# RWKV attention and squared-ReLU FFN: the first chunk's loads with pieces outermost, a permuted identity, and ten fillers at the start

## The chip, the cores and the metric

The kernel runs on one core of a Trainium2 chip. The metric is device time in microseconds, the median of several executions. The core has TensorE (matmuls, in the profile PE and PEld), VectorE (DVE), ScalarE (ACT), GpSimd (POOL) and SyncE (SP), which issues most DMAs; sixteen DMA engines move the data.

## The reference

Per batch and head a state of 48 by 48 runs over 768 tokens; its output, laid out as tokens by 384, goes through a feed-forward network (FFN) with a squared ReLU. All is float32; there are 4 batches and 8 heads.

```
for t in range(S):
    cur = einsum('bhd,bhe->bhde', u[None] * k_t, v_t)
    y[:, :, t] = einsum('bhd,bhde->bhe', r_t, state + cur)
    state = w_t[:, :, :, None] * state + einsum('bhd,bhe->bhde', k_t, v_t)
x = y.transpose(0, 2, 1, 3).reshape(B * S, H * D)
out = square(maximum(x @ w_in, 0)) @ w_out      # 384 -> 2048 -> 384
```

## The kernel before

The tokens go in six chunks of 128. A unit is one chunk of one batch, so chunk 0 has four units. For each unit `attention` forms running products of w (the scans, L509), scaled r and k, scores, and the output; `ffn` then takes a chunk of all four batches through 16 slices of the hidden dimension (first matmuls L688, second L706). Weights come from DRAM in 8 groups (`load_w`, L391 and L393) and are split into a high and a low part by ScalarE, VectorE and GpSimd (`split_w`, L404 to L425).

In the first chunk w, k and r are loaded one batch at a time (L444): twelve loads, each with 128 partitions of 8 tokens x 48 numbers, 1536 bytes. The partition is 16 * head + piece, where a piece is 8 consecutive tokens. TensorE turns each loaded tile into rows of head dimension by columns of tokens (`turn`, L497): 16 matmuls per tile, the loaded data stationary, the columns of an identity moving, picked per pair of heads (`pick`). A profile shows each of them as two records. The three turns of the first unit are queued in the order w, k, r; behind them on TensorE stands a turn of the second unit. VectorE's scans read the turned w, its products at L529 and L520 the turned k and r, and the rest of its queue follows in order. In later chunks the data is turned on VectorE (L459) instead, and spread by DMAs (L469).

Everything after the setup is added to a `Plan`, which simulates the engines with given costs, orders the steps by their simulated starts, and then writes them out in that order. No step is reordered by the hardware: each engine works its queue off in order. At most eight DMAs are in flight in the plan. Before a TensorE step that the simulation has waiting, `run` puts fillers (L750): transposes of the identity into a free bank, whose number is computed from the simulated idle time (`IDLE`, `s.fill`). Fillers take no time in the simulation.

The first planned TensorE step is the transpose of u (L359), which has no simulated dependence, but on the chip waits for a small DMA that ScalarE's queue issues (L357). The first turn comes after it. The lines of the count are:

```
if at < self.IDLE[0] and bank is not None:
    s.fill = max(0, int((at - max(idle, self.IDLE[1]) - self.IDLE[2]) / self.IDLE[3])), bank
```

Of the kernel before, what the change touches and what calls it, by code (L numbers as in the profile page):

```python
# [9 lines left out]
F32 = mybir.dt.float32  # L10
# [25 lines left out]
class Plan:  # L36
# [8 lines left out]
    QUEUES = {"sp": 0.5, "actq": 0.36}  # L45
    LANES, RUNS, SLACK, START = 8, 2300, 2.0, 1.4
    SWITCH, KEEP = 0.094, 1.0
    IDLE = (110.0, 2.8, 0.3, 0.12)
    filler, RULE = None, 1

    def __init__(self):
        self.steps, self.pools, self.last, self.readers = [], {}, {}, {}
# [26 lines left out]
    def order(self):  # L79
# [13 lines left out]
        while len(out) < len(self.steps):  # L93
# [40 lines left out]
            if unit == "pe":  # L134
                bank = next((x[1] for p in ("a", "hp") for x in self.pools.get(p, ()) if x[0] <= idle), None)
                if at < self.IDLE[0] and bank is not None:
                    s.fill = max(0, int((at - max(idle, self.IDLE[1]) - self.IDLE[2]) / self.IDLE[3])), bank
            wait[s.engine].remove(s)
# [43 lines left out]
        return sorted(out, key=lambda s: (s.at, s.n))  # L182

    def run(self):
        for s in self.order():
            for _ in range(s.fill[0] if self.filler else 0):
                self.filler(s.fill[1])
            s.fn()
# [39 lines left out]
def kernel(  # L228
# [12 lines left out]
    V, A, G, T = nc.vector, nc.scalar, nc.gpsimd, nc.tensor  # L241
    A.preload_act_table_set("natural_log_exp_and_others")
    B, H, S, D = r.shape
# [3 lines left out]
    NP = H // 2  # L247
# [10 lines left out]
    def place(name, shape, dtype, at):  # L258
        n = 1
        for x in shape[1:]:  # L260
            n *= x
        if at is None:
            nc.alloc_sbuf_tensor(name + "_place", [128, n], F32)
            at = placed[name] = nc.sbuf_base - 4 * n
        return nc.alloc_sbuf_tensor_at(name, shape, dtype, offset=at).ap()
# [13 lines left out]
    spare, spare2 = placed[f"ro{NG - 2}"], placed[f"ri{NG - 2}"]  # L279
    sel = place("sel", [HP, KT, J], F32, spare)  # L280
    last_y = [place(f"ly{i}", [HP, C], F32, spare + 768 + 512 * i) for i in range(2)]
    first_v = [place(f"v0{i}", [128, H * J], F32, at) for i, at in enumerate((spare + 1792, spare + 3840, spare2, spare2 + 2048))]
    gts = []
    for i in range(3):
        g = place(f"g{i}", [128, 2, 512], F32R, None)
# [9 lines left out]
    ident = const.tile([128, 128], F32, name="ident")  # L295
# [14 lines left out]
    TB = C // 16  # L310
# [34 lines left out]
    for q in range(KT):  # L345
        for h, i in enumerate(SIDE[q]):
            x = sel[:, q, h * D:h * D + PC]
# [19 lines left out]
    P.add("pool", 1.0, RANKS.unit(0, 3, "load") + 0.5, lambda: G.tensor_scalar(out=un, in0=un, scalar1=-1.0, scalar2=None, op0=ALU.mult), w=["un"])  # L367
    for t in Ss:
        V.memset(t, 0.0)

# [58 lines left out]
    def attention(c, b, rank):  # L431
        ss = slice(c * C, c * C + C)
# [4 lines left out]
        if b % 2 == 0:  # L437
            st = Slot("st" if c else "st0", n)
            both[n] = d = {"st": st}
            after = [both[n - 1]["z"]] if n > 2 else []  # L440
            for b0 in (b, b + 1) if c == 0 else ():
                for i, src in ((0, w), (2, k), (1, r)):
                    def load(i=i, src=src, b0=b0):
                        nc.sync.dma_start(out=st.tile.rearrange("s (t b x) -> s t b x", t=3, b=2)[:, i, b0 - b, 0:TB * D],  # L444
                                          in_=src[b0, :, ss, :].rearrange("h (a s) d -> h a (s d)", s=TB))
                    P.add("sp", 0.65, rank("load") + b0 - b, load, w=[(st, b0 - b, i)], after=after, runs=128)
            for b0, m in ((b, 2),) if c else ():
                for i, src in ((0, w), (2, k), (1, r)):
                    def load(i=i, src=src, b0=b0, m=m):
                        nc.sync.dma_start(out=st.tile.rearrange("s (t b h d) -> s t (b h) d", t=3, b=2, h=H)[:, i, (b0 - b) * H:(b0 - b + m) * H, 0:D],  # L450
                                          in_=src[b0:b0 + m, :, ss, :].rearrange("b h s d -> s (b h) d"))
                    P.add("sp", 1.05 * m, rank("load") + b0 - b, load, w=[(st, x, i) for x in range(b0 - b, b0 - b + m)], after=after, runs=128 * H * m)
            if c > 0:
                z = Slot("st", n)

                def blocks(i):
                    zt = z.tile.rearrange("a (u t p q i) -> a u t p q i", u=2, t=3, p=NP, q=3)
                    sv = st.tile.rearrange("s (t b p q x) -> s t b p q x", t=3, b=2, p=NP, q=3)
                    V.transpose(out=zt[:, i].rearrange("a t p q i -> a t (p q) i"),  # L459
                                in_=sv[:, :, i].rearrange("s t p q x -> s t (p q) x"))  # L460

                for i in range(2):
                    d["z"] = P.add("dve", 1.3, rank("z"), lambda i=i: blocks(i), r=[(st, i, x) for x in range(3)], w=[(z, i)])
                used = [s for s in P.steps if any(type(x) is tuple and x[:2] == ("pt", n % 2) for x in s.keys)]

                def spread(q, x, m, to, tb):
                    zz = z.tile.rearrange("a (w q i) -> a q w i", w=6 * NP, q=3)
                    pz = pts[n % 2].rearrange("a u t p s -> a (u t p) s")
                    nc.sync.dma_start(out=pz[to:to + m, :, 32 * tb:32 * tb + 32], in_=zz[32 * tb + x:32 * tb + x + m, q])  # L469

                for q, x, m, to in ((0, 0, 32, 0), (1, 0, 16, 32), (1, 16, 16, 64), (2, 0, 32, 80)):
                    for tb in range(4):
                        P.add("sp", 0.62 * m / 32, rank("pt"), lambda a=(q, x, m, to, tb): spread(*a), r=[(z, 0), (z, 1)],
                              w=[("raw", n, q, x, tb)], after=used, runs=24 * m)
        d = both[n]
# [7 lines left out]
                                                              in_=v[b, :, ss, :].rearrange("h s d -> s h d")), w=[vt], runs=128 * H)  # L483
        if c == 0:
            home = (["o0", "o1", "o2"], ["o3", "hp", "hp"], ["o2", "o3", "a"], ["o2", "o3", "a"])[b]
            ps = {}
            for i, h in zip((0, 2, 1), (home[0], home[2], home[1])):
                ps[i] = Slot(h) if h in ("hp", "a") else ("ob", int(h[1]))

                def turn(i=i):  # L490
                    to = tl(ps[i]).rearrange("a (p x y) -> a p x y", p=NP, y=TB)
                    rows = st.tile.rearrange("s (t b x) -> s t b x", t=3, b=2)[:, i, ui]
                    pick = ident.rearrange("s (p j x) -> s p j x", p=NP, j=2)
                    for y in range(TB):
                        for j in range(2):
                            n = (J, D)[j]
                            T.matmul(to[j * J:j * J + n, :, :, y], rows[:, y * D:y * D + n], pick[:, :, j], start=True, stop=True, skip_group_check=True)  # L497
                P.add("pe", 1.0, rank("turn"), turn, r=[(st, ui, i)], w=[ps[i]], mode=3)

            def tl(x):  # L500
                return x.tile if type(x) is Slot else obs[x[1]]
            src = lambda t: tl(ps[t]).rearrange("a (p s) -> a p s", p=NP)[0:HP]
        else:
            src = lambda t: pt[:, t]
# [133 lines left out]
        for nm, sl, y, hi, lo, k1, c1, c2 in outs:  # L638
            P.add("act", c1, rank(nm), lambda y=y, hi=hi: A.activation(hi(), y(), AF.Copy, scale=-1.0), r=[sl], w=[k1 + ("hi",)], after=freed)  # L639
            P.add("dve", c2, rank(nm), lambda y=y, hi=hi, lo=lo: V.scalar_tensor_tensor(  # L640
                out=lo(), in0=y(), scalar=-1.0, in1=hi().bitcast(F32), op0=ALU.mult, op1=ALU.subtract), r=[sl, k1 + ("hi",)], w=[k1 + ("lo",)])
# [86 lines left out]
    x = 0  # L728
    for c in range(NC):
# [4 lines left out]
        order = [(f, bs) for bs in ((0, 2), (2, B)) for f in range(HALF[c])] + [(f, (0, B)) for f in range(HALF[c], NF)]  # L734
# [23 lines left out]
    with tc.If(any_bad > 0):  # L758
        with tc.tile_pool(name="dram", bufs=1, space=bass.MemoryType.DRAM) as dr, \
                tc.tile_pool(name="slow", bufs=1) as sl:  # L760
            TB = 8
# [6 lines left out]
            with tc.For_i(0, S, TB) as t0:  # L768
# [17 lines left out]
                for b in range(B):  # L786
                    nc.sync.dma_start(
                        out=xd[b * S:b * S + S].rearrange("s (h d) -> h s d", d=D)[:, ds(t0, TB)],
                        in_=ys[b * H:b * H + H])
# [58 lines left out]
```

## Time and profile before

| what | us |
|---|---|
| median of three timed executions | 547.25 (546.74 to 547.51) |
| span of the profiled execution, first to last instruction | 545.6 |
| busy TensorE (PE) | 530.7, 97% |
| busy VectorE | 351.2, 64% |
| busy ScalarE | 300.4, 55% |
| busy GpSimd | 92.8, 17% |

The profile gives the profiled execution by its span; a whole time of that one execution isn't listed, so the span is set beside the median, 1.65 us above it. The page cuts the span into 40 slices and gives each engine's busy share in tenths. TensorE is at 9 in all slices but the first and the last, fillers included. VectorE and ScalarE are near 8 or 9 in the first ten or so, and lighter later. DMA is at 9 and below in the first third. In rows of the timeline the first number is the start, the second the duration, then engine, line, operation, tiles and count; a bracket gives the idle time before and what ended it. A line of SPq is the issue of a DMA, not its transfer.

### The profile page before, as it was taken

The page shows a single profiled execution, that of the slowest core. Times are in us where ns is not written, and L with a number is a line of the kernel's source. Part 1 is how long each engine was busy: PE and PEld are TensorE (multiplying, and loading weights), DVE is VectorE, ACT ScalarE, POOL GpSimd, SP SyncE. Part 2 cuts the span into 40 slices and gives each one's busy share as a digit, 9 for nine tenths or more (in the row PEclk, how much of TensorE's full clock was granted, in tenths as well). Part 3 has the DMA queues.
Part 4 walks back from the last instruction along what each step waited for, and adds up shares of the span by engine and source line. Part 5 has one row for each costly group of instructions (what it writes and reads, how often), then busy time and mean ns, then how long its engine had stood idle before and what let it go on. Part 6 is the DMA issues. An engine that isn't in the chain of part 4 may idle for free.

```text
span 545.6 us, 11056 instructions
## 1 busy us (share of the span) xinstructions
PE 530.7 (97%) x4250; PEld 470.7 (86%) x4250; DVE 351.2 (64%) x652; ACT 300.4 (55%) x728; POOL 92.8 (17%) x111
## 2 busy tenths in 40 slices
PE   5999999999999999999999999999999999999994
PEld 5888998889998989888888888889888998999994
DVE  2999888989796959696784684948443333333331
ACT  2887989895766675483834377464333232333221
POOL 2036533634030311212030030200000000000000
PEclk9999999999999999999999999999999999999997
DMA  4999695657947587674577155770011000000001
GB/s 150 231 246 234 136 257 143 138 106 110 183 75 113 115 89 124 82 155 59 91 119 110 26 104 101 123 95 1 0 44 44 1 0 1 29 31 0 1 0 62
DMA packets 195817, 50.91 MB, mean 93 GB/s; under 512 B 183984, under 2 KB 190640, under 8 KB 195760
## 3 DMA queue, kind: packets, MB, share of 16 engines
q1 hardware_dynamic: 195440, 49.76, 46.7%
q8 instruction: 35, 0.57, 0.5%
q10 hardware_dynamic: 320, 0.40, 0.2%
q14 instruction: 22, 0.18, 0.1%
HBM read 31.66 MB, written 4.72 MB: 67 GB/s over the span
## 4 chain that ended last, share of the span: by engine, by line
PE 90%; DMA 5%; SPq 1%; DVE 1%; ACT 1%; issue 0%; DVEq 0%
PE hp L688 38%; PE ob L706 38%; PE a L607 4%; PE a L567 4%; DMA ri<-in_moe_w_in_dram 3%; PE a L599 2%; PE a L659 2%; PE a L579 1%; DMA st<-in_k_dram 1%; SPq L444 1%; DMA st<-in_r_dram 1%; ACT m L556 0%; SPq L391 0%; PE a L621 0%; DVE m L571 0%
## 5 line engine op out<-in xcount | busy, mean ns | idle before, releaser
L706 PE MATMUL ob<-wo,g 128*128 128x384 f32 x1152 | 226.9, 341 | 0.0
L688 PE MATMUL hp<-x,wi 128*128 128x512 f32 (+1 forms) x1062 | 222.8, 355 | 0.0
L706 PEld LDWEIGHTS ob<-wo,g 128*128 128x128 f32 x1152 | 200.1, 188 | 10.3 <-issue 2.6
L688 PEld LDWEIGHTS hp<-x,wi 128*128 128x128 f32 x1062 | 173.9, 188 | 26.5 <-DVE g L700 1.0
L693 ACT ACTIVATE t<-hp 128x512 f32<-128x512 f32 (+1 forms) x118 | 61.1, 518 | 122.3 <-PE hp L688 107.7
L697 DVE SCALAR_TENSOR_TENSOR hp<-hp,t 128x512 f32<-128x512 f32 (+1 forms) x96 | 58.1, 606 | 90.9 <-ACT t L693 90.7
L700 DVE TENSOR_TENSOR g<-hp,g 128x512 fp32r<-128x512 f32 (+1 forms) x118 | 68.9, 584 | 38.0 <-ACT g L699 37.1
L699 ACT CAST g<-hp 128x512 fp32r<-128x512 f32 (+1 forms) x118 | 59.7, 506 | 52.9 <-DVE hp L697 52.5
L556 ACT ACTIVATE m<-ident,beta 128x128 f32<-128x128 f32 x192 | 60.6, 397 | 1.2 <-DVE beta L541 1.1
L571 DVE COPY_PREDICATED m<-caus,a 128x512 f32<-128x512 uint8 x48 | 34.1, 732 | 6.2 <-PE a L567 5.0
L640 DVE SCALAR_TENSOR_TENSOR x<-a,x 112x128 fp32r<-112x128 f32 (+2 forms) x64 | 20.6, 344 | 24.6 <-ACT x L639 23.0
L509 DVE TENSOR_TENSOR_SCAN pt<-pt,zero 112x128 f32<-112x128 f32 x80 | 30.0, 421 | 4.0 <-DMA pt<-st 3.5
L639 ACT ACTIVATE x<-a 112x128 fp32r<-112x128 f32 (+2 forms) x64 | 18.5, 323 | 21.0 <-PE a L607 16.6
L567 PEld LDWEIGHTS a<-pt 48*128 48x128 f32 x384 | 24.0, 187 | 6.7 <-issue 2.9
L567 PE MATMUL a<-pt 48*128 48x128 f32 x384 | 28.9, 285 | 0.7 <-DVE pt L546 0.7
L607 PE MATMUL a<-m,v 128*48 128x128 f32 (+1 forms) x384 | 26.9, 279 | 0.4 <-DVE m L571 0.2
L538 POOL TENSOR_TENSOR st<-st 128x384 f32<-128x384 f32 x20 | 20.9, 1050 | 37.4 <-DVE st L459 37.4
L459 DVE STREAM_TRANSPOSE st<-st 128x1152 f32<-128x1152 f32 x20 | 26.3, 1350 | 0.0
L607 PEld LDWEIGHTS a<-m,v 128*48 128x48 f32 (+1 forms) x384 | 19.8, 128 | 5.7 <-issue 4.2
L525 POOL COPY Ec<-pt 112x4 f32<-112x4 f32 x20 | 6.0, 300 | 103.8 <-DVE pt L509 103.8
L425 POOL TENSOR_TENSOR wi<-q,wi 128x768 fp32r<-128x768 f32 x8 | 16.7, 2087 | 28.5 <-ACT wi L424 23.3
L540 POOL TENSOR_TENSOR st<-st,un 128x384 f32<-128x384 f32 x20 | 21.3, 1071 | 1.3
(95 smaller groups left out, 428.2 us busy)
## 6 DMA issues: line engine op xcount, KB each, us to landing
pt<-st SPq DMA_DIRECT2D x80, 96.0 KB
ro<-in_moe_w_out_dram SPq DMA_DIRECT2D x8, 768.0 KB
v<-in_v_dram SPq DMA_DIRECT2D x24, 192.0 KB
st<-in_w_dram SPq DMA_DIRECT2D x10, 384.0 KB
st<-in_k_dram SPq DMA_DIRECT2D x10, 384.0 KB
st<-in_r_dram SPq DMA_DIRECT2D x10, 384.0 KB
pt<-st SPq DMA_DIRECT2D x80, 48.0 KB
out_dram<-q SPq DMA_DIRECT2D x20, 192.0 KB
```

The costliest lines, as they stand in the source:

```text
L459: V.transpose(out=zt[:, i].rearrange("a t p q i -> a t (p q) i"), in_=sv[:, :, i].rearrange("s t p q x -> s t (p q) x"))
L509: lambda p=p: V.tensor_tensor_scan(out=pt[:, 0, p], data0=src(0)[:, p], data1=zero.broadcast_to([HP, C]), initial=1.0, op0=ALU.mult, op1=A ...
L556: A.activation(mv(j)[:, p], ident, AF.Copy, scale=beta.tile[:, 2 * p + j:2 * p + j + 1])
L567: T.matmul(mts[j].tile.rearrange("s (p t) -> s p t", p=NP)[:, p], pt[js, 2, p], pt[js, 1, p], start=True, stop=True)
L571: lambda j=j: V.copy_predicated(out=mv(j), mask=caus.unsqueeze(1).broadcast_to([128, NP, C]), data=mts[j].tile.rearrange("s (p t) -> s p t ...
L607: T.matmul(spot(p)[to:to + n + D], vt.tile[:, o - n:o + D], mv(j)[:, p], start=(c == 0 and p == SPLIT), stop=True, skip_group_check=True)
L688: T.matmul(hp.tile[:, 0:n], wi[f][:, wl, kt], xT[:, kt, xl, xs], start=(m == 0), stop=(m == 3 * KT - 1))
L693: P.add("act", 0.5 if full else 0.28, rank("g"), lambda: A.activation(t(), h(), AF.Relu), r=[hp], w=[(g, 1)])
L697: P.add("dve", 0.61 if full else 0.33, rank("g"), lambda: V.scalar_tensor_tensor(out=h(), in0=h(), scalar=0.0, in1=t(), op0=ALU.max, op1=A ...
L699: P.add("act", 0.53 if full else 0.31, rank("g"), lambda: A.copy(out=hi(), in_=h()), r=[hp], w=[(g, 0)])
L700: P.add("dve", 0.61 if full else 0.33, rank("g"), lambda: V.tensor_tensor(out=lo(), in0=h(), in1=hi().bitcast(F32), op=ALU.subtract), r=[h ...
L706: T.matmul(obs[b][:, 0:DM], g.tile[0][:, gl, o:o + C], wo[f][:, wl], start=(f == 0 and m == 0), stop=(f == NF - 1 and m == 2))
```

## The change

The first chunk's loads walk the source with the 16 pieces outermost and the 8 heads inside, so that the partition becomes 8 * piece + head. The turns pick their columns from `perm`, a copy of the identity with its columns permuted to match; it is made once by VectorE in the setup and lies in memory that a late weight group uses afterwards. Ten fillers are put ahead of the first planned step. The time from which idle time counts for fillers goes from 2.8 to 5.3 us of the simulation.

```
-    IDLE = (110.0, 2.8, 0.3, 0.12)
-    filler, RULE = None, 1
+    IDLE = (110.0, 5.3, 0.3, 0.12)
+    filler, RULE, WARM = None, 1, 10
...
     def run(self):
-        for s in self.order():
+        order = self.order()
+        for _ in range(self.WARM if self.filler else 0):
+            self.filler(self.pools["a"][0][1])
+        for s in order:
...
+    perm = place("perm", [128, 128], F32, spare2 + 4096)
...
+    V.tensor_copy(out=perm.rearrange("s (h a) -> s h a", h=H), in_=ident.rearrange("s (a h) -> s h a", h=H))
...
                         nc.sync.dma_start(out=st.tile.rearrange("s (t b x) -> s t b x", t=3, b=2)[:, i, b0 - b, 0:TB * D],
-                                          in_=src[b0, :, ss, :].rearrange("h (a s) d -> h a (s d)", s=TB))
+                                          in_=src[b0, :, ss, :].rearrange("h (a s) d -> a h (s d)", s=TB))
...
-                    pick = ident.rearrange("s (p j x) -> s p j x", p=NP, j=2)
+                    pick = perm.rearrange("s (p j x) -> s p j x", p=NP, j=2)
```

## The prediction

> **What bounds the kernel now.** I read the page first, for the shape of the span, then the busy times of long stretches.
>
> ```profile
> span 545.6 us, 11056 instructions
> ...
> PE   5999999999999999999999999999999999999994
> ...
> DVE  2999888989796959696784684948443333333331
> ...
> DMA  4999695657947587674577155770011000000001
> ```
>
> ```profile
> 45.00:110.00 65.00, 64.88 (x519) 57.45 (x520) 56.08 (x89) 58.25 (x139) 29.58 (x18) 1.00 0.77 173
> 110.00:300.00 190.00, 190.00 (x1633) 169.33 (x1632) 147.78 (x301) 119.10 (x317) 39.98 (x52) 1.00 0.66 110
> 300.00:530.00 230.00, 230.00 (x1426) 202.87 (x1425) 110.77 (x189) 93.30 (x201) 11.02 (x13) 1.00 0.19 36
> ```
>
> The columns after the stretch are its length, PE, PEld, DVE, ACT and POOL busy with their counts, the granted clock, DMA share and GB/s. From 45 us to 530 us TensorE is busy in 484.88 of 485 us. That part is a solid block whose work the change does not touch, so the end moves by just as much as the block's beginning does. Everything is decided in the front, before 45 us. Its opening on TensorE and VectorE, in order of time (start, duration, line, and in brackets the idle time before):
>
> ```profile
> 5.72 0.23 PE L359 MATMUL hp<-ident,m 8*112 8x8 f32 x1 [5.72 <-DMA m<-in_u_dram]
> 5.88 3.89 PE L750 MATMUL a<-ident 128*128 128x128 f32 x17
> 9.70 4.54 PE L497 MATMUL ob<-ident,st 128*64 128x64 f32 x128
> ...
> 11.49 1.37 DVE L509 TENSOR_TENSOR_SCAN pt<-ob,zero 112x128 f32<-112x128 f32 x4 [8.60 <-PE ob L497]
> 13.42 0.69 DVE L529 TENSOR_TENSOR pt<-pt,ob 112x512 f32<-112x512 f32 x1 [0.57 <-PE ob L497]
> ...
> 44.85 1.34 PE L688 MATMUL hp<-x,wi 128*128 128x256 f32 x9
> ```
>
> TensorE waits for the little load of u until 5.72, runs 17 fillers (L750) and begins the first turn only at 9.70. VectorE's first scan waits 8.60 us for that turn. Was the data late too? The queue's issues say:
>
> ```profile
> 1.68 0.63 SPq L444 DMA_DIRECT2D st<-in_k_dram  x1
> 2.35 0.60 SPq L444 DMA_DIRECT2D st<-in_r_dram  x1
> ...
> 4.91 0.66 SPq L481 DMA_DIRECT2D v<-in_v_dram  x1
> 5.99 0.66 SPq L444 DMA_DIRECT2D st<-in_w_dram  x1
> 7.27 0.60 SPq L444 DMA_DIRECT2D st<-in_k_dram  x1
> 7.91 1.00 SPq L444 DMA_DIRECT2D st<-in_r_dram  x1
> 8.96 1.08 SPq L444 DMA_DIRECT2D st<-in_w_dram  x1
> ...
> 11.87 6.43 SPq L391 DMA_DIRECT2D ri<-in_moe_w_in_dram  x6
> ```
>
> ```profile
> 2.35 4.90 DMA st<-in_r_dram
> ...
> 13.83 7.91 DMA ri<-in_moe_w_in_dram
> ```
>
> The chain of waits has r of the first batch issued at 2.35 and landed at 7.25; w and k, issued before it on the same queue, come earlier. So at 9.70 all three inputs of the first unit lay there, the last for 2.4 us. The fillers, not the data, held the turn back. That is the main finding.
>
> After this start the front is a closely packed sequence on VectorE, with DMA saturated behind it:
>
> ```profile
> 2.00:22.00 20.00, 15.59 (x309) 14.93 (x311) 10.18 (x25) 8.38 (x27) 1.57 (x9) 1.00 0.68 186
> 14.00:46.00 32.00, 30.54 (x503) 26.82 (x499) 31.20 (x52) 24.64 (x63) 10.50 (x10) 1.00 0.99 245
> 22.00:46.00 24.00, 23.23 (x340) 19.85 (x335) 23.85 (x37) 17.83 (x43) 10.31 (x9) 1.00 1.05 261
> ```
>
> VectorE is busy 31.20 of the 32 us from 14 to 46. Its sequence starts with L509 and L529, so the whole sequence should slide by what those two gain, if DMA slides as far.
>
> **The change, part by part.** *Loads.* The 12 loads of L444 keep their bytes (192 KB) and their number; their outermost source dimension becomes 16 pieces in place of 8 heads.
>
> ```profile
> 4.00:5.00 1.00, 0.00 (x0) 0.00 (x0) 0.00 (x0) 0.00 (x0) 0.00 (x0) 1.00 0.50 160
> ...
> 8.00:9.00 1.00, 1.00 (x7) 1.00 (x6) 0.00 (x0) 0.00 (x0) 0.00 (x0) 1.00 0.98 271
> ...
> 10.00:11.00 1.00, 1.00 (x24) 1.00 (x22) 0.00 (x0) 0.00 (x0) 0.00 (x0) 1.00 0.59 171
> 11.00:12.00 1.00, 1.00 (x41) 1.00 (x39) 0.51 (x2) 0.00 (x0) 0.00 (x0) 1.00 0.52 192
> ```
>
> With these loads alone in flight the DMA share is 0.50 and 160 GB/s: eight of sixteen engines. When the load of v joins, whose outermost dimension is 128 tokens, it is 0.98 and 271. So the price of one load lies between 196.6 KB / 160 = 1.23 us (nothing changes) and half of it, 0.61 us (all sixteen); I take the half. The issue of one, 0.60, then becomes the pace.
>
> *The wait for u.* u's load shares the engines with w and k, which move about 393 KB ahead of it: 2.46 us at 160 GB/s, 1.23 us at double rate. The row at 5.72 becomes 5.72 - 1.23 = 4.5; the other bound is no gain, 5.72. I take 4.6, since the packets of the two are few.
>
> *Seventeen fillers out, ten in ahead of u.* The planner computes n = (at - max(idle, 2.8) - 0.3) / 0.12; n = 17 means at is about 5.2, and with 5.3 in the place of 2.8 n is 0. Later steps have idle above 5.3 (the first turn alone is costed at 1.0), so the other 64 of the 81 fillers remain (rows below), and so does the order, in which fillers have no time. The 17 took 3.89 us, 0.23 each. The ten need only the identity:
>
> ```profile
> L750 PE MATMUL a<-ident x53: 272/273/475, 5.9 to 30.2; 128*128 128x128 f32 x53
> L750 PE MATMUL hp<-ident x28: 270/273/329, 32.0 to 58.6; 128*128 128x128 f32 x28
> ...
> 1.25 0.29 POOL masks.py:199 TENSOR_SCALAR_AFFINE_SELECT ident<-ident 128x128 f32<-128x128 f32 x1
> ...
> 1.90 0.90 DVE L369 MEMSET S<- 112x208 f32 x4
> ...
> 2.74 0.15 DVE L343 CAST caus<-m 128x128 uint8<-128x128 f32 x1
> ```
>
> The identity is ready at 1.54, ten at 0.23 end at 3.9: inside the wait for u, 0.6 us before it ends. Were u there at once, they would cost up to those 2.3 us.
>
> *The permuted identity.* One copy of 128x128 with strided reads, not in the trace. The nearest row is the 128x128 cast, 0.15 us; the far bound is one scan, 1.37 / 4 = 0.34. I take 0.2, nearer the cast. It ends at about 3.1, hidden by VectorE's 8.60 us of idleness and 1.7 us before the turn needs it. Without this cover it would delay the turn by its 0.2. The turn's matmuls keep shapes and number.
>
> *Sum at the first turn.* It starts at about 4.6 + 0.16 = 4.8 in place of 9.70: 4.9 us earlier. Of this the fillers give 3.9 and u's earlier landing 1.1, rounding aside.
>
> *What the clock takes back.* The first of the 128 turn records run slowly: the windows above show 24 records in 10 to 11 us and 41 in the next. The clock column reads 1.00 in both, so the slow part is seen in the counts alone. The w turn (32 of the 128) ends where the scan starts: 11.49 - 9.70 = 1.79 slow; the other three take (14.24 - 11.49) / 3 = 0.92 each. The speed-up comes near 11.0, 5.2 us after TensorE's first work at 5.72. If the same delay counts from the ten fillers' start at 1.7, it comes at 6.9: w turn 4.8 to 6.55, k to 7.7, r to 8.6, and L529 starts at 8.7: 4.7 us earlier than 13.42. If the pause of 0.6 us after the fillers sets the clock back, all three turns run slowly: 4.8 + 3 x 1.75 = 10.05, L529 at 10.1, only 3.3 earlier. I take 4.2, nearer the first, since the pause is short beside the work before and after it.
>
> By the Trainium skill ("TensorE: Matmul & The Clock Gate", Part 4: PE-mode transpose) transposes do not count as work for the clock, so the ten fillers would be useless as warm-up; by that the gain would be the 3.3. This trace disagrees: 1.3 us after the first turn record the rate is already 41 per us, and ahead of it lay nothing but u's transpose and fillers.
>
> *The SP queue and the weights.* The gaps before the issues at 5.99 and 7.27 (0.41 and 0.62) wait for the landing of earlier loads, and the issues at 7.91 and 8.96 are long by 0.40 and 0.48. All four go when loads land sooner, so the first weight load is issued 1.9 us earlier, at about 10.0: that is the low bound of DMA's shift. High bound: 20 us at a share of 0.68 hold 13.6 us of full work, so 6.4 at most. I take 4.5, for the eight engines' backlog is what stretches the weights' six issues to 6.43. Compute's 4.2 is then just covered.
>
> *Total.* 545.6 - 4.2 = 541.4 span. The profile's span is 1.65 us under the 547.25 median of the timed runs; put on that, 547.25 - 4.2 = 543.0.
>
> **The rivals.**
> *DMA sets the front's pace.* One wait inside speaks for it, ACT held for the second weight:
>
> ```profile
> 25.61 0.94 ACT L404 ACTIVATE q<-ro 128x768 f32<-128x768 f32 x1 [0.49 <-DMA ro<-in_moe_w_out_dram]
> ...
> 36.64 1.96 DVE L412 SCALAR_TENSOR_TENSOR q<-ri,q 128x768 uint32<-128x768 uint32 x1
> ...
> L412 DVE SCALAR_TENSOR_TENSOR q<-ri,q x8: 944/959/2471, 25.8 to 107.3; 128x768 uint32<-128x768 uint32 x8
> ```
>
> If the saturated stretch from 22 us slides by 1.9 only, so does the block: 547.25 - 1.9 = 545.3. Against it stands the idle DMA capacity before 22 us.
>
> *The loads still use eight engines.* Then u stays at 5.72 and the weights stay where they are; ACT at 25.61 starts no earlier than its DMA, and only its 0.49 of slack is left, or nothing: 546.9, no change. The v load's 0.98 speaks against it. By the Trainium skill ("DMA: Bandwidth & Descriptors", Why a DMA increments its semaphore by 16 and not by 1) the slowest dimension of both sides must divide by the number of engines, at most 16; that gives 16 here and agrees with the 0.50 for 8 heads.
>
> *More than forecast.* If u lands before the fillers end, the turn starts at 4.1 and all but the first runs fast: w to 5.9, k and r to 7.7, L529 at 7.8, 5.6 earlier; with the 0.49 of ACT's wait 6.1: 541.2.
>
> *Slower.* Weight splitting on VectorE (L412, L417) takes 0.95 us alone and up to 2.47 beside GpSimd's subtraction: the row at 36.64 took 1.96. Earlier weights could bring GpSimd's work beside the five splits ahead of 45 us that now run undisturbed. The price is up to 1.5 each, 7.6 in all: 547.25 - 4.2 + 7.6 = 550.7. It outweighs the gain from 4.2 us on, that is from three of the five. Against it: GpSimd follows ACT and VectorE, so their spacing slides as one.
>
> **How the numbers follow.** Forecast 0.70 (543.0, its own range 542.2 to 544.2 from shifts of 5.0 to 3.1), DMA's pace 0.16, eight engines 0.05, more 0.05, slower 0.04. The range runs from 541.2, the larger gain, to 545.4, DMA's pace; outside are the eight engines, the slower case and the far edge of DMA's pace. A measurement of this kernel can tell about 0.2%, 1.1 us, from no change. Faster holds the forecast, the larger gain and nearly all of DMA's pace: 0.90. Within 0.2%: 0.06. Slower: 0.04.
>
> **What would show it.** DMA share between 3 and 6 us near 1.0 and about 300 GB/s; L359 at 4.4 to 5.0; ten L750 from 1.7 to 3.9 and none between L359 and L497; the first scan at 6.6, L529 between 8.7 and 10.1; the first FFN matmuls (L688), 44.9 before, near 40.7, and TensorE without gaps from then on. The forecast is wrong if VectorE or ACT shows new waits for weights between 15 and 40 us, or if the solid block begins earlier but tears open.

## The result and the profile after

The changed kernel takes 545.69 us (median of 14) against 548.04 us before (median of 14 beside it): a ratio of 0.9944, 95% interval 0.9927 to 0.996, or 3.1 us less with an interval of 2.2 to 4.0; the two medians alone differ by 2.35. Two more sets of executions gave 0.9943 (0.9925 to 0.996) and 0.9951 (0.9932 to 0.997).

The profiled execution is one of the longer ones of the changed kernel (546.6 us), so its span shows less than the median. The opening on TensorE, on VectorE and then the start of the block of FFN matmuls (timeline of the changed kernel; start, duration, line, in brackets the idle time before; L363 was L359, L502 was L497, L514 was L509, L534 was L529, L693 was L688, L755 was L750):

```profile
span 544.8 us, 11043 instructions
...
1.60 2.39 PE L755 MATMUL a<-ident 128*128 128x128 f32 x10 [1.60 <-POOL ident masks.py:199]
5.62 0.23 PE L363 MATMUL hp<-ident,m 8*112 8x8 f32 x1 [1.62 <-DMA m<-in_u_dram]
5.77 6.42 PE L502 MATMUL ob<-perm,st 128*64 128x64 f32 x128
...
7.80 1.37 DVE L514 TENSOR_TENSOR_SCAN pt<-ob,zero 112x128 f32<-112x128 f32 x4 [4.78 <-PE ob L502]
11.28 0.69 DVE L534 TENSOR_TENSOR pt<-pt,ob 112x512 f32<-112x512 f32 x1 [2.12 <-PE ob L502]
...
23.16 0.69 DVE L534 TENSOR_TENSOR pt<-pt,ob 112x512 f32<-112x512 f32 x1 [0.89 <-ACT pt L533]
...
24.34 0.93 ACT L409 ACTIVATE q<-ro 128x768 f32<-128x768 f32 x1
...
43.91 1.33 PE L693 MATMUL hp<-x,wi 128*128 128x256 f32 x9
```

The first turn starts 3.9 us earlier than before (5.77 for 9.70), but its 128 records take 6.42 us in place of 4.54, and only 2.1 us are left at L534 (11.28 for 13.42). At the first FFN matmul 0.9 us are left (43.91 for 44.85).

The same stretches as before, in windows (length, PE, PEld, DVE, ACT, POOL busy with counts, clock, DMA share, GB/s):

```profile
4.00:5.00 1.00, 0.00 (x0) 0.00 (x0) 0.00 (x0) 0.00 (x0) 0.00 (x0) 1.00 0.94 290
...
10.00:11.00 1.00, 1.00 (x24) 1.00 (x23) 0.00 (x0) 0.62 (x2) 0.00 (x0) 1.00 1.11 281
11.00:12.00 1.00, 1.00 (x36) 1.00 (x32) 0.69 (x1) 0.00 (x0) 0.00 (x0) 1.00 1.13 267
...
18.00:19.00 1.00, 1.00 (x25) 1.00 (x25) 0.64 (x2) 1.00 (x4) 0.00 (x0) 0.55 1.06 340
19.00:20.00 1.00, 1.00 (x25) 1.00 (x23) 0.73 (x2) 1.00 (x4) 0.00 (x0) 0.50 1.21 249
20.00:21.00 1.00, 1.00 (x24) 1.00 (x22) 1.00 (x4) 0.99 (x4) 0.00 (x0) 0.50 1.05 252
21.00:22.00 1.00, 1.00 (x33) 1.00 (x30) 1.00 (x4) 0.00 (x0) 0.00 (x0) 0.75 1.16 240
```

```profile
2.00:22.00 20.00, 17.79 (x324) 17.06 (x324) 12.24 (x30) 9.53 (x30) 1.71 (x9) 0.91 1.07 255
...
110.00:300.00 190.00, 189.67 (x1631) 169.09 (x1630) 147.46 (x301) 118.76 (x316) 40.06 (x53) 1.00 0.66 109
300.00:530.00 230.00, 230.00 (x1426) 202.94 (x1425) 110.35 (x187) 92.78 (x201) 10.93 (x13) 1.00 0.18 36
```

Three things are to be seen. The loads now use all engines: a share of 0.94 and 290 GB/s where 0.50 and 160 stood, 1.07 from 2 to 22 us (the share of this view can pass 1) where 0.68 stood. TensorE is slow until past 11 us, at 24 records per us. The column of the granted clock reads 1.00 there too, but the first change of the clock that the trace holds is the speed-up at 11.27 us, so before it the counts are what to read. And from 18.1 to 21.5 us its granted clock is at one half once more; the missing shares, 0.45 + 0.50 + 0.50 + 0.25, make 3.4 us at half clock.

The SP queue (start and duration of each issue) no longer waits. The first weights are issued at 9.98, where 11.87 stood, and the six issues take 3.91 us, where they took 6.43:

```profile
4.75 0.59 SPq L486 DMA_DIRECT2D v<-in_v_dram  x1
5.39 0.70 SPq L449 DMA_DIRECT2D st<-in_w_dram  x1
...
9.98 3.91 SPq L396 DMA_DIRECT2D ri<-in_moe_w_in_dram  x6
14.33 0.39 SPq L398 DMA_DIRECT2D ro<-in_moe_w_out_dram  x1
```

The theory from here on, A: the fillers, not the data, held the first turn; the loads matter because without them the weights would come too late for the earlier start. B: DMA sets the front's pace. Theory P on the clock: TensorE's 1.6 us pause between the ten fillers and u undoes them.

### The profile page after: what moved, and what is told of

It is laid out like the page before. It is cut to its first block, busy times and chain, and to the rows that moved or that the text cites. A ratio compares the mean times of both kernels' runs of the same rounds, so it can differ in the third digit from the quotient of the medians.

```text
span 544.8 us, 11043 instructions
## 1 busy us (share of the span) xinstructions
PE 532.6 (98%) x4243; PEld 472.8 (87%) x4243; DVE 351.4 (65%) x653; ACT 300.3 (55%) x728; POOL 94.5 (17%) x111
## 4 chain that ended last, share of the span: by engine, by line
PE 81%; SPq 6%; DMA 5%; DVE 5%; ACT 1%; issue 1%; DVEq 0%
PE hp L693 34%; PE ob L711 34%; SPq L474 4%; PE a L612 3%; DMA ri<-in_moe_w_in_dram 3%; PE a L572 3%; PE a L604 2%; PE a L664 2%; DMA pt<-st 1%; SPq L449 1%; DVE st L464 1%; PE a L584 1%; SPq L455 1%; SPq L486 1%; DVE pt L551 1%
## 5 line engine op out<-in xcount | busy, mean ns | idle before, releaser
L693 PE MATMUL hp<-x,wi 128*128 128x512 f32 (+1 forms) x1062 | 222.7, 355 | 0.0
L693 PEld LDWEIGHTS hp<-x,wi 128*128 128x128 f32 x1062 | 174.1, 188 | 26.2 <-issue 0.9
L514 DVE TENSOR_TENSOR_SCAN pt<-pt,zero 112x128 f32<-112x128 f32 x80 | 30.0, 422 | 5.7 <-DMA pt<-st 5.5
L572 PEld LDWEIGHTS a<-pt 48*128 48x128 f32 x384 | 23.9, 187 | 6.5 <-issue 3.2
L572 PE MATMUL a<-pt 48*128 48x128 f32 x384 | 28.7, 285 | 0.6 <-DVE pt L551 0.6
L530 POOL COPY Ec<-pt 112x4 f32<-112x4 f32 x20 | 7.4, 372 | 102.7 <-DVE pt L514 101.7
```

The costliest lines, as they stand in the source:

```text
L514: lambda p=p: V.tensor_tensor_scan(out=pt[:, 0, p], data0=src(0)[:, p], data1=zero.broadcast_to([HP, C]), initial=1.0, op0=ALU.mult, op1=A ...
L572: T.matmul(mts[j].tile.rearrange("s (p t) -> s p t", p=NP)[:, p], pt[js, 2, p], pt[js, 1, p], start=True, stop=True)
L693: T.matmul(hp.tile[:, 0:n], wi[f][:, wl, kt], xT[:, kt, xl, xs], start=(m == 0), stop=(m == 3 * KT - 1))
```

## The experiments

Each set was timed beside the kernel before on the same chip; a single profile belongs to each. The changed kernel itself was timed on the chips of the loads alone, the fillers alone, the eighteen fillers and the thirteen; for the other sets (no fillers at the start, early u with ten fillers, and both with five fillers in the gap) only the ratios to the kernel before can be compared with it. "Start of the block" is the first FFN matmul (L688 before, 44.85).

**The changed kernel again.** Twice, on two chips.

> The changed kernel once more, as the measure for the others on this chip. Both theories: 545.7 beside 548.0 before, ratio 0.9944 within its interval 0.9927 to 0.996. If the clock's state early in the span is a matter of luck, its first fast stretch begins at another time than 11.3 us, and the half-clock stretch of 3.4 us at 18 us is absent or elsewhere.

> The changed kernel as the measure for the two others of this call: ratio 0.9944 within 0.9927 to 0.996 on every theory; its executions spread over 2 to 3 us, as the clock's first fast stretch and a half-clock stretch after it fall differently.

Measured: 544.63 us, ratio 0.9943 (0.9925 to 0.996), and 545.24 us, 0.9951 (0.9932 to 0.997). The first profile has no half-clock stretch, the second has one, from 17.8 to 21.2 us. The windows and the block's start of the first, then L534 and the block's start of the second:

```profile
18.00:19.00 1.00, 1.00 (x42) 1.00 (x39) 0.65 (x2) 1.00 (x3) 0.00 (x0) 1.00 1.13 298
19.00:20.00 1.00, 1.00 (x42) 1.00 (x40) 1.00 (x3) 1.00 (x5) 0.00 (x0) 1.00 1.12 226
...
11.15 0.69 DVE L534 TENSOR_TENSOR pt<-pt,ob 112x512 f32<-112x512 f32 x1 [2.12 <-PE ob L502]
...
42.43 2.38 PE L693 MATMUL hp<-x,wi 128*128 128x256 f32 x18
```

```profile
11.21 0.69 DVE L534 TENSOR_TENSOR pt<-pt,ob 112x512 f32<-112x512 f32 x1 [2.09 <-PE ob L502]
...
43.82 2.38 PE L693 MATMUL hp<-x,wi 128*128 128x256 f32 x18
```

With nearly the same L534 (11.15 and 11.28) the block starts at 42.43 without the stretch and at 43.91 with it; the spans are 542.8 and 544.8. In the profile with the stretch the turns of the second pair ran at 25 records per us in place of 42, and VectorE waited 0.89 us at 23.16 for ScalarE's reading of one of them. The other set's profile agrees: from L534 to the block it takes 32.61 us with its stretch, the one of the section before 32.63 with its own, and the one without a stretch 31.28. So this stretch costs about 1.35 us at the block's start, and it falls on some executions and not on others.

The mean granted clock that goes with every execution shows how often. The four profiled executions with such a stretch, of all kernels here, have a mean of 0.992 to 0.994, the nine without one 0.995 to 0.998. (Every profile also ends with 2.2 to 5.5 us at half clock, after the last matmul.) By that mark, 6 of the 31 executions of the changed kernel hold a stretch: five of the first 14, with a median of 546.34 us against 544.61 for the other nine, none of 11, and one of six. The kernel before has them too: 31 of the 52 executions whose clock is listed are at 0.994 or less, and they are slower by 0.8, 0.5 and 0.2 us in the medians of three sets. Where in the span these fall is known for the profiled ones alone.

**The loads alone.**

```
-    IDLE = (110.0, 5.3, 0.3, 0.12)
-    filler, RULE, WARM = None, 1, 10
+    IDLE = (110.0, 2.8, 0.3, 0.12)
+    filler, RULE, WARM = None, 1, 0
```

> The loads with pieces outermost and the permuted identity, but the fillers as before (17 before the first turn, none at the very start). Theory A (the fillers held the first turn, the loads did not): the first turn still starts near 9.7, and only the 0.5 us of ScalarE's wait for the second weight is won: ratio 0.999 to 1.000. Rival B (DMA set the front's pace): about 1.9 us, ratio 0.9965.

Measured: 548.31 us, ratio 1.000 (0.9981 to 1.0019). Timeline of TensorE:

```profile
5.59 0.23 PE L363 MATMUL hp<-ident,m 8*112 8x8 f32 x1 [5.59 <-DMA m<-in_u_dram]
5.74 3.89 PE L755 MATMUL a<-ident 128*128 128x128 f32 x17
9.56 4.81 PE L502 MATMUL ob<-perm,st 128*64 128x64 f32 x128
```

Seventeen fillers still hold the turn to 9.56, and all that DMA gained comes to nothing. Rival B is out: faster loads by themselves are worth nothing here.

**The fillers alone** (the loads with heads outermost, the plain identity, no copy of it).

```
-    V.tensor_copy(out=perm.rearrange("s (h a) -> s h a", h=H), in_=ident.rearrange("s (a h) -> s h a", h=H))
...
-                                          in_=src[b0, :, ss, :].rearrange("h (a s) d -> a h (s d)", s=TB))
+                                          in_=src[b0, :, ss, :].rearrange("h (a s) d -> h a (s d)", s=TB))
...
-                    pick = perm.rearrange("s (p j x) -> s p j x", p=NP, j=2)
+                    pick = ident.rearrange("s (p j x) -> s p j x", p=NP, j=2)
```

> Ten fillers first and none between the transpose of u and the first turn, the loads as before with heads outermost. Theory A: the first turn starts at 5.9, L529's product of r 2 us earlier than before, but ScalarE then waits for the second weight until 25.6, so that about 0.5 to 1 us remains: ratio 0.998 to 0.999; with e1 it gives less than the whole change, because the two parts need each other. Rival B: no gain, ratio 1.000. Rival C (the fillers alone are the whole gain, no need of the loads): ratio 0.9944.

Measured: 547.50 us, ratio 0.998 (0.9962 to 0.9998), 1.1 us less by the ratio and 0.6 by the medians. VectorE's product of r, then ScalarE's first two readings of raw weights, in the timeline (lines stand one earlier here):

```profile
10.62 0.69 DVE L533 TENSOR_TENSOR pt<-pt,ob 112x512 f32<-112x512 f32 x1 [1.21 <-PE ob L501]
...
22.98 0.91 ACT L408 ACTIVATE q<-ri 128x768 f32<-128x768 f32 x1 [2.07 <-DMA ri<-in_moe_w_in_dram]
24.92 0.92 ACT L408 ACTIVATE q<-ro 128x768 f32<-128x768 f32 x1 [0.51 <-DMA ro<-in_moe_w_out_dram]
...
44.52 2.40 PE L692 MATMUL hp<-x,wi 128*128 128x256 f32 x18
```

The product of r is 2.8 us earlier than before, and then ScalarE waits 2.07 and 0.51 us for weights that have not landed. The wait has gone from fillers to DMA. (This profile also has a half-clock stretch, from 26.3 to 29.8 us, so the block's start at 44.52 is not the price of these waits alone.) Zero for the loads and 1.1 us for the fillers against 3.1 us for both: the two parts need each other, as theory A has it.

**Eighteen fillers at the start**, so that TensorE has no pause before u. Two sets, on two chips.

```
-    filler, RULE, WARM = None, 1, 10
+    filler, RULE, WARM = None, 1, 18
```

> The changed kernel with 18 fillers at the start in place of ten, so that TensorE has no pause of 1.6 us before u lands at 5.6. Theory P (the pause made the ten fillers useless for the clock): the clock is fast by 8.4 us at the latest where it was 11.3, the product of r at L534 comes 1.5 to 2.5 us earlier, and the time is about 544.2, ratio 0.992. Rival Q (only real matmuls wake the clock, or fillers count even with a pause): the same as the changed kernel, ratio 0.9944, clock fast near 11.

> The kernel with 18 fillers again, beside the changed kernel on one chip. Theory P: 1 to 2 us faster than the changed kernel, ratio to the kernel before 0.989 to 0.992, spread under 2 us, clock fast by 8.4 us. Rival: the first measurement was a favourable draw of six executions; then the ratio is 0.994, as the changed kernel's.

Measured: 543.18 us, ratio 0.9906 (0.9882 to 0.9931), and 543.96 us, 0.993 (0.9909 to 0.9952). The changed kernel beside them had 544.63 and 545.24, so this version is lower by 1.4 and 1.3 us; each pair of intervals overlaps, but the two sets agree. Opening, then windows, of the first:

```profile
1.61 4.10 PE L755 MATMUL a<-ident 128*128 128x128 f32 x18 [1.61 <-POOL ident masks.py:199]
5.64 0.26 PE L363 MATMUL hp<-ident,m 8*112 8x8 f32 x1
5.83 4.49 PE L502 MATMUL ob<-perm,st 128*64 128x64 f32 x128
...
9.51 0.69 DVE L534 TENSOR_TENSOR pt<-pt,ob 112x512 f32<-112x512 f32 x1 [0.57 <-PE ob L502]
...
41.21 2.38 PE L693 MATMUL hp<-x,wi 128*128 128x256 f32 x18
```

```profile
6.00:7.00 1.00, 1.00 (x22) 1.00 (x23) 0.00 (x0) 0.25 (x2) 0.00 (x0) 1.00 1.00 280
7.00:8.00 1.00, 1.00 (x40) 1.00 (x38) 0.43 (x2) 0.00 (x0) 0.00 (x0) 1.00 1.16 220
```

The turn starts at the same time as with ten fillers, but TensorE is fast from 7 us on in place of 11, and the product of r comes 1.8 us earlier (9.51 for 11.28). In the second set's profile the clock is fast already in the window from 6 to 7 us (33 records). This bears theory P out, and it answers a page too. The Trainium skill ("TensorE: Matmul & The Clock Gate", Part 4: PE-mode transpose) says that transposes do not count as work for the clock; here nothing but transposes ran until 5.8, and the clock rose within 1.2 us of the first other matmul, so the trace disagrees.

**No fillers at the start.**

```
-    filler, RULE, WARM = None, 1, 10
+    filler, RULE, WARM = None, 1, 0
```

> The changed kernel without the ten fillers at the start. Theory P (the 1.6 us pause after them had made them useless for the clock): no difference to the changed kernel, ratio 0.993 to 0.996, clock fast near 11 us. Rival R (they counted in part): the clock later by up to one stretch of 3.4 us, 1 us or more slower than the changed kernel, ratio 0.996 to 0.998.

Measured: 544.56 us, ratio 0.9921 (0.9896 to 0.9946). Timeline:

```profile
5.46 0.23 PE L363 MATMUL hp<-ident,m 8*112 8x8 f32 x1 [5.46 <-DMA m<-in_u_dram]
5.62 6.15 PE L502 MATMUL ob<-perm,st 128*64 128x64 f32 x128
...
10.96 0.69 DVE L534 TENSOR_TENSOR pt<-pt,ob 112x512 f32<-112x512 f32 x1 [1.95 <-PE ob L502]
```

The interval holds 0.9944, and the turns are as slow as with ten fillers (6.15 us, 6.42). The ten fillers of the change bring nothing; the pause after them undoes them, and rival R is out. What the change gains on TensorE comes from the seventeen fillers that it takes away.

**Early u, with ten and with thirteen fillers at the start.** The zeroing of u's tile and its two DMAs go ahead of the other zeroing on VectorE.

```
-    for t in st0:
-        V.memset(t[:, :, :, TB * D:], 1.0)
...
-    V.memset(ut, 0.0)
...
+    u8 = P.pools["m"][1][1][0:H, 0:HP]
+    V.memset(u8, 0.0)
+    for j in range(2):
+        nc.scalar.dma_start(out=u8[:, j * J:j * J + D], in_=u)
+    for t in st0:
+        V.memset(t[:, :, :, TB * D:], 1.0)
+    V.memset(ut, 0.0)
...
-    u8 = P.pools["m"][1][1][0:H, 0:HP]
-    V.memset(u8, 0.0)
-    for j in range(2):
-        nc.scalar.dma_start(out=u8[:, j * J:j * J + D], in_=u)
```

> The changed kernel with the zeroing of u's tile and u's two DMAs moved to the front of the setup, so that they are issued near 1.1 us in place of 1.9. u then lands near 4.3 in place of 5.5, and the ten fillers, which end at 4.0, touch the work behind them. Theory P with u as the gate of the first turn: first turn at 4.5, clock fast by 8.4 us at the latest, L534 at 8.5 to 9.5. But the weights then come late: with 18 fillers ScalarE already waited 0.8 us for the second weight. So the gain over 18 fillers is small, 0 to 0.7 us: ratio 0.989 to 0.991. Rival S (nothing else binds): the full 1.3 us more, ratio 0.988. Rival T (u is not the gate, its landing is set by traffic): first turn still at 5.6, ratio 0.994.

> Early u with 13 fillers at the start in place of ten: they end at 4.6 in place of 4.0, after u has landed (4.1 to 4.3), so TensorE has no pause at all before the turns. Theory P (any pause before the turns makes the clock's start a matter of luck, and that is the 4.6 us spread of early u with ten): spread as narrow as with 18 fillers, 1.5 us, median 542.5 to 543.2, ratio 0.9885 to 0.990. Rival W (the spread of early u comes from the weights' late landing or from half-clock stretches later on): spread of 3 us or more again, ratio near 0.992.

Measured with ten: 544.77 us, ratio 0.9923 (0.9893 to 0.9952), executions from 542.11 to 546.73. With thirteen: 544.02 us, 0.9942 (0.9921 to 0.9963), from 542.6 to 547.07. The profile with ten is the fastest of all (span 540.3). First the issue of u's load in the changed kernel, then this kernel's rows, then a window of it and one of the kernel with thirteen:

```profile
1.94 1.04 ACTq L361 DMA_DIRECT2D m<-in_u_dram  x2
```

```profile
1.07 0.92 ACTq L340 DMA_DIRECT2D m<-in_u_dram  x2
...
4.29 0.23 PE L363 MATMUL hp<-ident,m 8*112 8x8 f32 x1 [0.29 <-DMA m<-in_u_dram]
4.45 4.38 PE L502 MATMUL ob<-perm,st 128*64 128x64 f32 x128
...
39.79 2.38 PE L693 MATMUL hp<-x,wi 128*128 128x256 f32 x18
```

```profile
5.00:6.00 1.00, 1.00 (x35) 1.00 (x32) 0.00 (x0) 0.00 (x0) 0.00 (x0) 1.00 0.93 274
```

```profile
7.00:8.00 1.00, 1.00 (x30) 1.00 (x28) 1.00 (x4) 0.00 (x0) 0.00 (x0) 1.00 1.19 202
```

Issuing u's load 0.9 us earlier brings its transpose, and the first turn with it, 1.3 us forward. So u is the gate of the first turn, and its issue decides when it lands; rival T is out. But the medians do not follow the profile: in neither set is early u shown to be better than the changed kernel. Removing the last pause did not narrow the spread, so that reading of it (theory P for the spread) fell, and what makes these executions so unequal is open. Half-clock stretches do not explain the slowest of the two sets: 546.73 and 547.07 have mean clocks of 0.996 and 0.997. The speed-up itself does move: TensorE is fast from 5.4 us in the profile with ten, where 0.29 us of idleness stand between the fillers and u, and from 7.7 in the one with thirteen, where none do. Among equal kernels the profiles show it move by 0.6 us (10.9 to 11.5 in three of the changed kernel) and 0.8 (6.3 and 7.1 in two with 18 fillers); whether that makes the spread here is not shown.

**Five fillers in the gap before the first scores**, and the same with early u. `run` puts them out ahead of the step of L572 in the first unit.

```
+            for _ in range(s.more if self.filler else 0):
+                self.filler(self.pools["a"][0][1])
             s.fn()
...
-        P.add("pe", 1.0, rank("mt"), scores, r=RK + KK, w=mts, mode=1, claim=Ms)
+        scored = P.add("pe", 1.0, rank("mt"), scores, r=RK + KK, w=mts, mode=1, claim=Ms)
+        scored.more = 5 if c == b == 0 else 0
```

> The changed kernel with five more fillers ahead of the first scores (L572), where TensorE idles for 0.6 us near 15.5. Theory U (the half-clock stretch at 18 us that some executions show comes from too little TensorE work in the 3.4 us before it): no such stretch between 14 and 25 us in the profile, the slower third of the executions goes, median 0.3 to 0.7 us lower than the changed kernel, ratio 0.9930 to 0.9940. Rival V (it comes from something else): the same spread and median as the changed kernel.

> Early u and the five fillers together. Theory: the two add up as far as the weights allow; ratio 0.988 to 0.991, the fastest of these kernels or equal to 18 fillers. Rival: the five fillers delay the scores where the gap has closed; 0.3 us slower than early u alone.

Measured: 545.13 us, ratio 0.9934 (0.9908 to 0.9959), and with early u 544.28 us, 0.9917 (0.9888 to 0.9945). Neither profile has a half-clock stretch, but seven of the eleven other profiles, the one of before among them, have none either, and the medians are not shown to be lower. None of the six executions with five fillers and u as it was has a mean clock under 0.995, but none of the six without fillers at the start has either. Inconclusive on what brings the stretch on; as an improvement, no.

## Why the prediction was right or wrong

The time: 3.1 us gained, forecast 4.2; 545.69 lies outside 541.2 to 545.4 by the plain median, but the kernel before, timed again beside it, had 548.04; the ratio puts the change at 544.2 on the forecast's base (0.9944 x 547.25), inside the range and at the edge of the forecast's own; the difference of the two medians, 2.35, puts it at 544.9, inside the range and outside the forecast's own. The range held because it had room for the slow clock; two terms of the sum did not come, and the signs set down for the opening failed with them (u's transpose at 5.62 for 4.4 to 5.0, the first scan at 7.80 for 6.6, L534 at 11.28 for 8.7 to 10.1, the block at 43.91 for 40.7).

**Held.** The block's end moves with its beginning: span less start of L693 is 500.8 us before, 500.8 after, 500.3 in the second profile after, 500.0 with 18 fillers and 500.5 with early u. The fillers held the first turn (loads alone: 1.000). No filler stands between L363 and L502, and 64 later ones stand as they were. The loads spread over all engines (0.94 for 0.50), so the eight-engine rival is out. The first weights are issued 1.9 us earlier, as summed, and ScalarE's reading of the second weight, at 24.34, no longer waits. The permuted identity cost nothing: VectorE idled 4.78 us before its first scan.

**Wrong: u's earlier landing.** The step "The row at 5.72 becomes 5.72 - 1.23 = 4.5" was worth 1.1 us in the sum and was 0.1 (5.62; 5.49 in the second profile). Its bound "no gain, 5.72" was nearly the true one. Halving the time of the bytes ahead of u left it where it was, and issuing it 0.9 us earlier moved it by 1.3. The packed trace has u's own packets: the last ends at 5.13 us before, 4.54 in the changed kernel and 3.22 with early u, but the last signal of its completion comes at 5.58, 5.48 and 4.15. So the faster loads brought u's data 0.6 us forward and its signal 0.1. What holds the signal back was not settled.

**Wrong in size: what the clock takes back.** I took 4.2 between 4.7 and 3.3 because "the pause is short". With u still late the pause was 1.62 us, and all three turns ran slowly: 5.77 + 3 x 1.75 = 11.0, and L534 started at 11.28. The slow end of the term was right, and the later u came off it as well: 13.42 - 11.28 = 2.1 us at L534.

**Not foreseen: the half-clock stretch.** It takes back about 1.35 us of those 2.1 in the executions that have it. The profile before has none, though by their mean clocks more than half of that kernel's listed executions do. The kernel before was also slower on the whole than its profiled execution (median 548.04 with 14 executions, 547.25 with the first three), which is why the ratio shows more than the two profiles, 545.6 and 544.8, do.

**Rivals.** DMA's pace does not bind in the changed kernel, since ScalarE waits for no weight there; it would bind with the fillers alone (2.07 us), and it is back as the next limit with 18 fillers. There the second weight lets ScalarE go on at 21.94, 3.7 us earlier than the 25.61 of before; the sum had taken 4.5 for DMA's shift. A turn as early as forecast would thus have run into the weights. From L534 to the block this profile takes 31.70 us, 0.4 more than the 31.28 above:

```profile
21.94 0.95 ACT L409 ACTIVATE q<-ro 128x768 f32<-128x768 f32 x1 [0.81 <-DMA ro<-in_moe_w_out_dram]
```

The slower rival did not come: on VectorE the splits before 45 us slid with the rest.

## What to carry to other kernels

Where filler work keeps an engine awake, compare the end of the fillers with the landing of the data: fillers that outlast it are the wait, and loads made faster behind them are worth nothing until they go. Two parts of a change can each be worth little and together much, when one removes a wait and the other keeps the next one from taking its place. Let warm-up work reach up to the real work: ten transposes with 1.6 us of idleness behind them did no more than none, while in one profile 0.29 us did not undo them.

## What the runs showed of the hardware that was not expected

TensorE came to full speed 3.4 to 6.05 us after its work began, in all thirteen profiles: between 5.4 and 7.7 for work that went on from 1.6 (with at most 0.29 us of idleness), between 9.3 and 11.5 for work from 5.5 to 5.9, whether ten transposes had ended 1.5 us or more before it or not. In four of the thirteen the granted clock fell back to 0.50 for 3.41 us: from 18.1 in the changed kernel's profile, 17.8 in the last one of that kernel, 16.5 in the second one with 18 fillers (in the row below), and 26.3 with the fillers alone. In the first three TensorE's busy share stood at 1.00 when the clock fell; in the last it had been nearly idle from 24.3 to 25.9. The falls come 6.83, 6.83, 10.24 and 17.07 us after the speed-up, that is 2, 2, 3 and 5 times 3.41. The Trainium skill ("TensorE: Matmul & The Clock Gate", What's actually happening) gives a free-running window of 3.413 us; the length and the spacing agree, and that the window is not tied to the kernel's start would fit that equal kernels differ. What in the work before it brings the fall on was not settled.

```profile
17.00:18.00 1.00, 1.00 (x24) 1.00 (x23) 1.00 (x3) 1.00 (x5) 0.00 (x0) 0.50 0.92 274
```
